# First attention batch: 512-query score tiles in single PSUM banks, remainders packed, row maxima over two banks

## The chip, the cores and the metric

One core of a Trainium2 chip runs the whole program. The metric is the device time of one execution in microseconds, the median over runs. The engines are named as the profile names them: PE (TensorE matmuls) with PEld (its weight loads), DVE (VectorE), ACT (ScalarE), POOL (GpSimd), SP (SyncE, which issues the DMAs). Each engine takes its instructions from one queue of its own, in order.

## What is computed

Thresholded attention over 4 batches, 8 heads, 576 positions and 64 dimensions, then two mixture-of-experts layers without routing, one after the other, over the 2304 positions.

```python
scores = scale * np.matmul(q, k.transpose(0, 1, 3, 2))
thresh = np.max(scores, axis=-1, keepdims=True) - tau
scores = np.where(scores >= thresh, scores, -1000000000.0)
scores = scores - np.max(scores, axis=-1, keepdims=True)
attn = np.exp(scores)
attn = attn / (np.sum(attn, axis=-1, keepdims=True) + 1e-09)
attn_out = np.matmul(attn, v)
...
h = x @ w_in                      # 512 -> 2048
g = P(h) / (Q(h) + 1e-06)         # cubic over quadratic in |h|
x = g @ w_out                     # 2048 -> 512
...
h = x @ w_in                      # second layer, 512 -> 2048
g = np.where(h >= 1, h, np.where(h <= -1, 0.0, (h + 1.0) ** 2 / 4.0))
out = g @ w_out
```

The weights arrive as 8-byte floats and have to be taken apart by integer instructions before they can be used.

## The kernel before

The program is a list of pieces of work, each with a priority (`at(when)`); a scheduler turns them into one fixed order for each engine. Three streams matter here.

**The first batch's attention** (`first_attention`, units at priorities -40 to -4). Heads are handled in four pairs. `prep_pair` loads and splits q and k of a pair into 16-bit halves and transposes them. `row_max` finds the largest score of each query: 128 queries by 512 keys per piece, two matmuls (L523, L524) into a PSUM bank and one DVE reduction (L527); then the rest pieces of 64 keys, then on nine columns the maximum is cut into three 16-bit pieces (`pcs`, L556), which PE transposes (L562) and ACT copies to `mrow` (L563). For pair 0 the pieces alternate between two PSUM tiles (tags `acc` and `s`); for the later pairs every piece uses the one bank `ph0`, and so do the three transposes. Then come nine score tiles per pair, keys on the partitions and all 576 queries along the row, as two halves of 288 in two banks (`transposed`): three matmuls per half (L579 to L581, the last of which subtracts the row maximum), an ACT instruction that marks what is under the threshold (L584, `low`), a matmul that subtracts the mark (L586), and the exponential (L587, `et`). Two score tiles exist (tags `s` and `acc`), each of two banks. The weighted sums of a tile (L596, two f32 matmuls, recorded as four) are issued one tile later, into the two banks `pv` and `ph1`; `take` copies them out in four or six ACT copies (L603, L604), and `divide` (L608 to L617) makes the result `xT` of the pair. The next pair's `row_max` is advanced beside the tiles, two units beside each of the first six tiles and one beside each of the others.

**The weights' conversion** (`convert`). 32 halves of weights, 16 for each layer, each 1 MB as read: a DMA into one of two `rw` buffers, three DVE instructions (L228 to L230), small matmuls for a bound (L253) with DVE and PE steps that make a scale (L254, L187, L188, L168 to L172), an ACT scaling and an ACT cast (L217, L208), four POOL subtractions (L212). The first layer's 16 halves have priorities -40 to -4, the second layer's 16 (`wh`) have -3 to 16.

**The layers** (`first_product`, `second_product`): 192 steps, 24 for each layer and batch, at priorities 0, 1, 2 and so on. One step is 24 matmuls (L846), some ten DVE and ACT instructions on 128 by 384 elements (`rational` L727 to L740 for the first layer, `quadratic` for the second), and three steps later 24 matmuls (L860). The first step needs `xT` of all four pairs. The attention of batches 1 to 3 (`attention`, scores L379 and L380, row instructions L425 and L387, sums L413) runs beside the steps, batch 1 from priority 16.5 on.

Eight PSUM banks exist: `aux`, `pv`, `ph0`, `ph1` (pool `ps_1`) and the two tiles of two banks `acc` and `s` (pool `ps_2`).

## Time and profile before

| what | us |
|---|---|
| runs: median (lowest to highest of 3) | 1267.02 (1266.43 to 1269.06) |
| the profiled execution's own time | 1266.28 |
| its span in the profile | 1264.5 |
| PE, PEld, DVE, ACT, POOL busy | 1096.8, 985.3, 1003.2, 824.5, 534.4 |
| last `xT` of the first batch written for step 0 (L617) | at 240.87 |

Times inside the program are counted from the start of the span. Busy time of an engine is what its instructions cover; the idle time of an engine that nobody waits for costs nothing, so each stage has to be read by itself. A granted clock of 1.00 is 2.4 GHz and one of 0.50 is 1.2 GHz; a mean between them is a mix of the two.

### The profile page before, as it was taken

The page shows a single profiled execution, that of the slowest core. Times are in us where ns is not written, and L with a number is a line of the kernel's source. Part 1 is how long each engine was busy: PE and PEld are TensorE (multiplying, and loading weights), DVE is VectorE, ACT ScalarE, POOL GpSimd, SP SyncE. Part 2 cuts the span into 40 slices and gives each one's busy share as a digit, 9 for nine tenths or more (in the row PEclk, how much of TensorE's full clock was granted, in tenths as well). Part 3 has the DMA queues.
Part 4 walks back from the last instruction along what each step waited for, and adds up shares of the span by engine and source line. Part 5 has one row for each costly group of instructions (what it writes and reads, how often), then busy time and mean ns, then how long its engine had stood idle before and what let it go on. Part 6 is the DMA issues. An engine that isn't in the chain of part 4 may idle for free.

```text
span 1264.5 us, 31682 instructions
## 1 busy us (share of the span) xinstructions
PE 1096.8 (87%) x12618; PEld 985.3 (78%) x12618; DVE 1003.2 (79%) x2371; ACT 824.5 (65%) x1473; POOL 534.4 (42%) x700
## 2 busy tenths in 40 slices
PE   2788778668788998999799999998889998999998
PEld 1454445567788887899688898997778998999997
DVE  7767977899997877789999766899997767897431
ACT  2476767668686677667676666777765766775332
POOL 3324546576553645421355454313454553222221
PEclk9797898779899999999999999999999999999999
DMA  7656657633427545933398548522784469006000
GB/s 206 221 171 213 231 193 248 239 114 98 117 73 234 114 98 100 241 124 84 73 225 193 94 91 205 178 53 58 214 185 76 102 148 243 14 2 237 32 14 26
DMA packets 220341, 176.40 MB, mean 139 GB/s; under 512 B 182048, under 2 KB 193312, under 8 KB 212000
## 3 DMA queue, kind: packets, MB, share of 16 engines
q1 hardware_dynamic: 220192, 174.36, 51.6%
q8 instruction: 99, 1.62, 0.5%
q14 instruction: 50, 0.41, 0.1%
HBM read 106.83 MB, written 21.50 MB: 101 GB/s over the span
## 4 chain that ended last, share of the span: by engine, by line
PE 37%; DVE 32%; DMA 11%; ACT 8%; issue 5%; POOL 5%; SPq 2%; DVEq 0%; ACTq 0%; POOLq 0%
PE ph L846 14%; PE acc L860 14%; DMA eT<-hl 6%; DVE e L387 3%; DVE sc L425 2%; PE pv L596 2%; DVE t L734 2%; DMA qkT<-qk 2%; PE pv L413 2%; DVE t L740 2%; DVE t L729 2%; DVE wt L229 2%; DMA rqk<-in_k_dram 2%; POOL hl L398 1%; DVE t L730 1%
## 5 line engine op out<-in xcount | busy, mean ns | idle before, releaser
L860 PE MATMUL acc<-gg,wc 128*128 128x192 f16 x4608 | 427.6, 247 | 16.7 <-DVE mye L188 8.4
L846 PEld LDWEIGHTS <-wc 128*128 128x128 f16 x4608 | 389.4, 99 | 30.0 <-DVE t L731 14.7
L860 PEld LDWEIGHTS <-wc 128*128 128x128 f16 x4608 | 383.7, 98 | 19.4 <-issue 17.8
L212 POOL TENSOR_TENSOR gg<-t,gg 128x384 f16<-128x384 f32 x192 | 187.6, 978 | 407.0 <-ACT gg L208 332.4
L846 PE MATMUL ph<-xT,wc 128*128 128x192 f16 x2304 | 220.1, 253 | 19.8 <-DVE t L731 15.3
L846 PE MATMUL ph<-yT,wc 128*128 128x192 f16 x2304 | 216.6, 246 | 2.3 <-DVE t L731 1.9
L398 POOL TENSOR_TENSOR hl<-e,hl 128x256 f16<-128x256 f32 x216 | 154.3, 735 | 0.0
L208 ACT CAST gg<-t 128x384 f16<-128x384 f32 x192 | 97.2, 508 | 83.9 <-DVE t L793 39.4
L387 DVE SCALAR_TENSOR_TENSOR e<-sc,nt,e 128x576 f32<-128x576 f32 x108 | 95.7, 886 | 33.0 <-ACT e L386 32.2
L792 DVE SCALAR_TENSOR_TENSOR t<-t,c 128x384 f32<-128x384 f32 x96 | 63.5, 662 | 72.6 <-ACT t L791 72.5
L386 ACT ACTIVATE e<-sc,nt,con 128x576 f32<-128x576 f32 x108 | 93.5, 866 | 7.2 <-POOL hl L398 0.2
L395 ACT CAST hl<-e 128x576 f16<-128x576 f32 x108 | 72.2, 669 | 35.6 <-DVE e L387 34.7
L727 ACT ACTIVATE t<-ph,sc 128x384 f32<-128x384 f32 x96 | 55.2, 575 | 60.8 <-PE ph L846 60.5
L791 ACT ACTIVATE t<-ph,c 128x384 f32<-128x384 f32 x96 | 64.0, 666 | 47.2 <-PE ph L846 46.7
L396 POOL TENSOR_TENSOR hl<-e,hl 128x64 f16<-128x64 f32 x108 | 40.0, 371 | 126.9 <-ACT hl L395 126.5
L413 PE MATMUL pv<-v,eT 128*128 128x65 f16 (+3 forms) x1680 | 70.7, 194 | 25.2 <-DMA eT<-hl 24.9
L425 DVE TENSOR_SCALAR_CACHE_REDUCE sc<-s 128x576 f32<-128x576 f32 x108 | 80.9, 749 | 13.3 <-PE s L380 12.8
L413 PEld LDWEIGHTS <-eT 128*128 128x128 f16 (+1 forms) x1680 | 62.9, 100 | 35.0 <-DMA eT<-hl 32.4
L732 ACT ACTIVATE t<-t,lc 128x384 f32<-128x384 f32 x96 | 67.9, 707 | 20.4 <-DVE t L729 19.8
L734 DVE SCALAR_TENSOR_TENSOR t<-t,ka,t 128x384 f32<-128x384 f32 x96 | 68.4, 713 | 13.9 <-ACT t L733 13.4
L212 POOL TENSOR_TENSOR wh<-wt,wh 128x256 f16<-128x256 f32 x64 | 60.6, 977 | 41.5 <-ACT wh L208 32.1
L212 POOL TENSOR_TENSOR wc<-wt,wc 128x256 f16<-128x256 f32 x64 | 55.4, 897 | 47.1 <-ACT wc L208 47.1
(233 smaller groups left out, 1901.5 us busy)
## 6 DMA issues: line engine op xcount, KB each, us to landing
wc<-scratch SPq DMA_DIRECT2D x56, 1024.0 KB, 5.9
rw<-in_moe_w_in_dram SPq DMA_DIRECT2D x16, 1024.0 KB, 5.9
rw<-in_moe_w_out_dram SPq DMA_DIRECT2D x16, 1024.0 KB, 5.6
scratch<-wc SPq DMA_DIRECT2D x8, 1024.0 KB, 5.8
scratch<-wh SPq DMA_DIRECT2D x16, 512.0 KB, 3.5
rqk<-in_q_dram SPq DMA_DIRECT2D x16, 256.0 KB, 3.0
rqk<-in_k_dram SPq DMA_DIRECT2D x16, 256.0 KB, 3.1
kT<-qkT SPq DMA_DIRECT2D x28, 144.0 KB, 2.4
```

What stands on the lines that cost most here:

```text
L208: A.copy(hi, src)
L212: G.tensor_tensor(lo[:, p], src[:, p], hi[:, p], op=ALU.subtract)
L386: A.activation(e, s, AF.Exp, bias=nb, scale=con[:, 0:1])
L387: V.scalar_tensor_tensor(e, s, th, e, op0=ALU.is_ge, op1=ALU.mult)
L395: A.copy(hi, e)
L398: G.tensor_tensor(lo_w[:, p], e[:, whole][:, p], hi[:, whole][:, p], op=ALU.subtract)
L413: T.matmul(pv[rows, 0:w], eT[:, c, cols], vv[:, h * NT + x if x < NT else H * NT + h, at : at + w], start=(n == 0), stop=(n == len(blocks) ...
L425: V.tensor_scalar(s, banks[:, 0:S], 1.0, -LARGEST, op0=ALU.mult, op1=ALU.max, accum_out=mx)
L732: A.activation(r, u, AF.Ln, bias=lc[:, 1:2], scale=lc[:, 0:1])
L734: V.scalar_tensor_tensor(s, s, ka[:, 0:1], r, op0=ALU.add, op1=ALU.mult)
L846: last = T.matmul(ph[:, f, :], w[:, wx, kt, f * P : (f + 1) * P], rhs, start=(n == 0), stop=(n == 3 * KT - 1))
L860: T.matmul(dst, w[:, wx, f, d * P : (d + 1) * P], gg[:, gx, f, :], start=(i == 0 and f == 0 and n == 0 and d % 2 == 0), stop=(i == NCH - 1 ...
```

## The change

Score tiles of the first batch now hold the first 512 queries in one bank. The last 64 queries of a head are computed for all its key tiles side by side in one bank, ahead of the nine main tiles (`_r` tiles: 320 columns for the first head, which carries the shared key tile, and 256 for the second). Their weighted sums go into the last 64 columns of that bank. The tags `s` and `acc` are taken once, as four banks: three rotate among the score tiles, the fourth serves `row_max`, which from pair 1 on alternates between it and `ph0`, the three transposes included. The weighted sums of the two heads go to `pv` and `ph1`, one bank each. A pair has ten program units in place of nine, so `N_FIRST` goes from 53 to 57.

```diff
         def bank(name):
-            if pr > 0:
-                return ps_1.tile([P, 512], F32, name=f"sm{pr}_{name}", tag="ph0")
             count[0] += 1
-            return ps_2.tile([P, 1024], F32, name=f"sm{pr}_{name}", tag="acc" if count[0] % 2 else "s")[:, 0:512]
+            if pr == 0:
+                return banks[count[0] % 4]
+            if count[0] % 2:
+                return banks[3]
+            return ps_1.tile([P, 512], F32, name=f"sm{pr}_{name}", tag="ph0")
...
-            pm = ps_1.tile([P, 512], F32, name=f"pmr{pr}_{c0}", tag="ph0")
+            pm = bank(f"m{c0}")
...
-    def transposed(pr, ab, t, data, n):
+    def transposed(name, parts, data, s):
...
+        w = sum(p[-1] for p in parts if p[1].start == 0)
+        for at, r, cols, c, of, n in parts:
+            dst, rhs = s[r, at : at + n], slice(of, of + n)
+            T.matmul(dst, kT[:, c, cols], q1[:, rhs], start=at == 0, stop=False, skip_group_check=True)
+            T.matmul(dst, kT2[:, c, cols], q1[:, rhs], start=False, stop=False, skip_group_check=True)
+            T.matmul(dst, less16[:, 0 : r.stop - r.start], mrow[:, rhs], start=False, stop=True, skip_group_check=True)
...
-        for z in range(2):
-            T.matmul(pv[z], w[r], e[r, z], start=first, stop=last)
+        T.matmul(pv, w[r], e[r], start=first, stop=last)
...
-        half = S // 2
-        for src, c0, c1, to in ((0, 0, ST, M), (0, ST, half, 0), (1, 0, half, half - ST)) if ab else ((0, 0, half, 0), (1, 0, half, half)):
-            c = slice(to, to + c1 - c0)
-            A.copy(d[h, c], pv[src][o, c0:c1])
-            A.copy(x[h, c], pv[src][h, c0:c1])
+        A.copy(d[h], pv[o])
+        A.copy(x[h], pv[h])
+
+    def rest(pr, e0, e1, pvs, vv, x, d):
+        for ab, dst in enumerate(pvs):
+            order = [NT, *range(NT)]
+            for n, t in enumerate(order):
+                e = e0 if ab == 0 or t == NT else e1
+                sums(dst, ab, pr, t, e[:, t * ST : (t + 1) * ST], vv, n == 0, n == NT)
+        for ab, pv in enumerate(pvs):
+            take(pv, ab, x[:, M:S], d[:, M:S])
...
+        two = [ps_2.tile([P, 1024], F32, name=f"front_{tag}", tag=tag) for tag in ("s", "acc")]
+        banks = [t[:, z * 512 : (z + 1) * 512] for t in two for z in range(2)]
...
+            for ab in range(2):
+                s = banks[n % 3]
+                pvs.append(s[:, M - ST : M])
+                n += 1
+                parts = sum((key_tile(ab, t, t * ST, 1) for t in range(NT + 1 - ab)), [])
+                es.append(transposed(f"{pr}_{ab}_r", parts, data, s))
+            held = [partial(rest, pr, *es, pvs, vv, x, d)]
+            next(rows, None)
+            yield
             for ab, t in [(0, t) for t in range(NT + 1)] + [(1, t) for t in range(NT)]:
-                e = transposed(pr, ab, t, data, n)
+                e = transposed(f"{pr}_{ab}_{t}", key_tile(ab, t, 0, 0), data, banks[n % 3])
...
-    N_FIRST = 17 + 9 * NP
+    N_FIRST = 17 + 10 * NP
```

What stands below are pieces of the fixed order of two engines. In the changed kernel the lines from 565 on are shifted: L565 is the `mrow` copy (was L563), L581 and L583 are `low` and `et` (were L584 and L587), L617 to L619 and L624 are `divide` (were L610 to L612 and L617).

ACT before, from the division of pair 0 (`rd_0`) to the first tile of pair 1 (`con_1` is a constant of pair 1; `wt` and `wc` are weights):

```order
L608 ACTIVATE rd_0_932<-d_0_594,least 128x576
L563 CAST mrow_262<-pmr_0_830 3x512
L217 ACTIVATE wt_3_0_722<-wt_3_0_722,pw_3_0_s 128x1024
L208 CAST wc_2_148<-wt_2_1_621 128x1024
L609 ACTIVATE rd_0_932<-rd_0_932 128x576
L217 ACTIVATE wt_3_1_879<-wt_3_1_879,pw_3_1_s 128x1024
L563 CAST mrow_262<-pmr_4_836 3x512
L208 CAST wc_3_149<-wt_3_0_722 128x1024
L208 CAST wc_3_149<-wt_3_1_879 128x1024
L563 CAST mrow_262<-pmr_8_842 3x128
L584 ACTIVATE low_0_0_954<-st_0_0_946,con_1_286 128x576
L584 ACTIVATE low_0_1_978<-st_0_1_970,con_1_286 128x576
```

ACT in the changed kernel, the same place, from the last `mrow` copy for pair 1 to the first tile of pair 1:

```order
L565 CAST mrow_262<-sm_m_793 3x128
L581 ACTIVATE low_1_1_842<-front_acc,con_0_175 128x512
L581 ACTIVATE low_1_2_852<-front_s,con_0_175 128x512
L208 CAST wc_2_148<-wt_2_1_659 128x1024
L217 ACTIVATE wt_3_0_798<-wt_3_0_798,pw_3_0_s 128x1024
L583 ACTIVATE et_1_1_841<-front_acc,con_0_175 128x512
L583 ACTIVATE et_1_2_851<-front_s,con_0_175 128x512
L217 ACTIVATE wt_3_1_859<-wt_3_1_859,pw_3_1_s 128x1024
L208 CAST wc_3_149<-wt_3_0_798 128x1024
L208 CAST wc_3_149<-wt_3_1_859 128x1024
L581 ACTIVATE low_1_3_893<-front_s,con_0_175 128x512
L581 ACTIVATE low_0_r<-front_acc,con_1_286 128x320
```

The `mrow` copies of pair 1 stood behind all of pair 0 and now stand ahead of its last three tiles; the first tile of pair 1 follows pair 0's last one directly, and the division of pair 0 comes behind it.

DVE before, the end of the first attention (`x_3` is pair 3's result; `wt_6_0` is a weight half of the second layer, the thirteenth of its sixteen) up to the first step's first instruction (L729):

```order
L188 TENSOR_REDUCE mw_5_0_3058<-pmmw_5_0_3059 128x1
L228 TENSOR_SCALAR wt_6_0_3304<-rw_6_0_3302 128x1024
L168 TENSOR_SCALAR f_w_137<-mw_5_0_3058 128x1
L617 SCALAR_TENSOR_TENSOR xT_0_258<-x_3_1612,v_s,xT_0_258 128x192
L229 SCALAR_TENSOR_TENSOR wt_6_0_3304<-rw_6_0_3302,wt_6_0_3304 128x1024
L617 SCALAR_TENSOR_TENSOR xT_1_259<-x_3_1612,v_s,xT_1_259 128x192
L171 TENSOR_SCALAR f_w_137<-f_w_137 128x1
L617 SCALAR_TENSOR_TENSOR xT_2_260<-x_3_1612,v_s,xT_2_260 128x192
L254 TENSOR_REDUCE mb_5_1_3145<-pg_5_1_3146 128x1
L230 SCALAR_TENSOR_TENSOR wt_6_0_3304<-rw_6_0_3302,wt_6_0_3304 128x1024
L172 RECIPROCAL pw_5_0_s<-f_w_137 128x1
L729 SCALAR_TENSOR_TENSOR t_0_0_0_1943<-t_0_0_0_1943,qc 128x384
```

DVE in the changed kernel, around the start of pair 3's division (`d_3`; `wt_7_1` is the last of all weight halves, `mv` belongs to the values of batch 1):

```order
L230 SCALAR_TENSOR_TENSOR wt_7_1_3570<-rw_7_1_3568,wt_7_1_3570 128x1024
L171 TENSOR_SCALAR f_w_137<-f_w_137 128x1
L300 TENSOR_REDUCE mv_3670<-rv_0_3671 128x1
L188 TENSOR_REDUCE mqke_0_3543<-pmmqke_0_3544 128x2
L617 SCALAR_TENSOR_TENSOR d_3_1544<-d_3_1544,rd_3_1786 128x576
L172 RECIPROCAL pw_7_0_s<-f_w_137 128x1
L259 TENSOR_REDUCE f_max_3448<-f_w_137 128x1
L159 TENSOR_SCALAR qk_0_f<-mqke_0_3543 128x2
L300 TENSOR_REDUCE mv_3670<-rv_1_3674 128x1
L254 TENSOR_REDUCE mb_7_1_3574<-pg_7_1_3575 128x1
L618 SCALAR_TENSOR_TENSOR d_3_1544<-d_3_1544,rd_3_1786 128x576
```

Before, the weight halves `6_0` (its last two instructions), `6_1`, `7_0` and `7_1` and the two L300 came behind the last `xT` of step 0; now all 32 halves and the L300 stand ahead of it.

## Rows read from the trace of the kernel before

**Rows 1.** Busy time by engine, granted clock and DMA around the first pair boundary.
```profile
92.00:105.00 13.00, 5.70 (x26) 2.53 (x23) 7.95 (x12) 12.60 (x20) 10.49 (x10) 0.59 0.66 194
```

**Rows 2.** The same view by stage: us, PE, PEld, DVE, ACT, POOL busy, PEclk, DMA, GB/s.
```profile
0.00:241.30 241.30, 164.42 (x986) 103.86 (x987) 185.50 (x404) 148.46 (x232) 110.54 (x133) 0.86 0.66 215
241.30:330.70 89.40, 63.95 (x622) 59.74 (x622) 86.33 (x174) 66.12 (x113) 52.97 (x56) 0.83 0.44 135
330.70:378.10 47.40, 42.65 (x532) 41.47 (x530) 45.76 (x104) 36.95 (x71) 26.30 (x27) 1.00 0.22 67
378.10:447.20 69.10, 62.27 (x812) 57.08 (x810) 54.13 (x145) 41.77 (x79) 32.05 (x48) 1.00 0.65 164
```

**Rows 3.** DVE's waits from 50 to 241.3: for whom, us in total, times, longest.
```profile
DVE wt L228 <- POOL wc L212: 7.7, 7, 2.5
DVE mw L188 <- PE pmmw L187: 6.2, 6, 2.3
DVE mx L527 <- PE sm L524: 5.6, 4, 3.4
...
DVE mb L254 <- PE pg L253: 3.9, 4, 1.5
...
DVE d L610 <- ACT rd L609: 3.5, 1, 3.5
DVE mx L527 <- PE sm_t L524: 3.0, 2, 2.5
DVE mx L527 <- PE sm_rt L524: 1.6, 2, 1.2
```

**Rows 4.** DVE by line, 50 to 241.3: count, busy us, mean ns of one, idle before.
```profile
L230 DVE SCALAR_TENSOR_TENSOR wt<-rw,wt 128x1024 int32<-128x1024 int32 x24 | 34.4, 1434 | 0.2
L229 DVE SCALAR_TENSOR_TENSOR wt<-rw,wt 128x1024 int32<-128x1024 int32 x25 | 32.8, 1310 | 0.2
L228 DVE TENSOR_SCALAR wt<-rw 128x1024 int32<-128x1024 int32 x25 | 19.1, 762 | 17.0 <-POOL wc L212 7.7 <-POOL wh L212 4.8 <-DMA rw<-in_moe_w_out_dram 3.6
L188 DVE TENSOR_REDUCE mw<-pmmw 128x1 f32<-128x128 f32 x23 | 6.5, 284 | 6.2 <-PE pmmw L187 6.2
...
L168 DVE TENSOR_SCALAR f_w<-mw 128x1 int32<-128x1 int32 x23 | 3.4, 149 | 0.4
```

**Rows 5.** DVE by line, 241.3 to 378.1, the same columns.
```profile
L300 DVE TENSOR_REDUCE mv<-rv 128x1 f32<-128x2048 f32 x2 | 4.5, 2272 | 0.0
...
L387 DVE SCALAR_TENSOR_TENSOR e<-sc,nt,e 128x576 f32<-128x576 f32 x4 | 3.2, 803 | 0.0
L425 DVE TENSOR_SCALAR_CACHE_REDUCE sc<-s 128x576 f32<-128x576 f32 x4 | 3.0, 745 | 0.0
...
L300 DVE TENSOR_REDUCE mv<-rv 128x1 f32<-128x512 f32 x2 | 1.3, 668 | 0.0
```

**Rows 6.** PE by line, 378.1 to 447.2 (attention of batch 1).
```profile
L413 PE MATMUL pv<-v,eT 128*128 128x65 f16 (+3 forms) x168 | 7.6, 194 | 5.1 <-DMA eT<-hl 5.1
L379 PE MATMUL s<-qkT 128*128 128x512 f16 (+3 forms) x26 | 6.9, 287 | 1.5 <-DVE sc L425 1.5
L380 PE MATMUL s<-kT,qkT 128*128 128x512 f16 (+3 forms) x26 | 5.3, 286 | 0.0
```

**Rows 7.** Timeline of DVE and ACT: start, us, instruction, idle before.
```profile
53.19 1.35 ACT L584 ACTIVATE low<-st,con 128x576 bf16<-128x576 f32 x2
...
197.22 1.37 ACT L584 ACTIVATE low<-st,con 128x576 bf16<-128x576 f32 x2
...
230.80 0.78 ACT L608 ACTIVATE rd<-d,least 128x576 f32<-128x576 f32 x1
...
240.87 0.41 DVE L617 SCALAR_TENSOR_TENSOR xT<-x,v_s,xT 128x192 f16<-128x192 f32 x1
```

**Rows 8.** ACT by line, 25 to 245: the two instructions of a score tile.
```profile
L584 ACT ACTIVATE low<-st,con 128x576 bf16<-128x576 f32 x36 | 25.7, 734 | 21.2 <-PE st L581 21.1
L587 ACT ACTIVATE et<-st,con 128x576 f32<-128x576 f32 x36 | 25.4, 738 | 9.3 <-PE st L586 9.3
```

More of the change, by code (lines that the diff above doesn't have):

```diff
@@ L507, in first_v, with row_max @@
         return vv
-    def row_max(pr, qT, kT, kT2, mrow):
+    def row_max(pr, qT, kT, kT2, mrow, banks):
         k1 = kT.rearrange("p c s -> p (c s)")
@@ L564, in row_max @@
         yield
-    def transposed(pr, ab, t, data, n):
+    def transposed(name, parts, data, s):
         con, qT, kT, kT2, mrow = data
-        name = f"{pr}_{ab}_{t}"
-        s = ps_2.tile([P, 1024], F32, name="st" + name, tag="acc" if n % 2 else "s")
-        s = s.rearrange("p (z n) -> p z n", z=2)[:, :, 0 : S // 2]
         q1 = qT.rearrange("p c s -> p (c s)")
-        tiles = [(ab, slice(0, P), slice(0, P), ab * (NT + 1) + t)]
-        if t == NT:
-            tiles = [(i, slice(i * ST, (i + 1) * ST), slice(i * ST, (i + 1) * ST), NT) for i in range(2)]
-        for i, r, cols, c in tiles:
-            for z in range(2):
-                dst, of = s[r, z], slice(i * S + z * S // 2, i * S + (z + 1) * S // 2)
-                T.matmul(dst, kT[:, c, cols], q1[:, of], start=True, stop=False)
-                T.matmul(dst, kT2[:, c, cols], q1[:, of], start=False, stop=False)
-                T.matmul(dst, less16[:, 0 : r.stop - r.start], mrow[:, of], start=False, stop=True)
-        e = mp.tile([P, 2 * W], F32, name="et" + name, tag="tp", bufs=N_TEMP)[:, 0:S].rearrange("p (z n) -> p z n", z=2)
-        low = mp.tile([P, 2, S // 2], BF16, name="low" + name, tag="poly", bufs=N_POLY)
@@ L584, in transposed @@
+        e = mp.tile([P, 2 * W], F32, name="et" + name, tag="tp", bufs=N_TEMP)[:, 0:w]
+        low = mp.tile([P, 2 * W], BF16, name="low" + name, tag="poly", bufs=N_POLY)[:, 0:w]
         A.activation(low, s, AF.Relu, bias=con[:, 3:4], scale=-STEEP)
-        for z in range(2):
-            T.matmul(s[:, z], minus, low[:, z], start=False, stop=True, skip_group_check=True)
+        T.matmul(s, minus, low, start=False, stop=True, skip_group_check=True)
         A.activation(e, s, AF.Exp, scale=con[:, 0:1])
@@ L588, in transposed, with key_tile @@
         return e
+    def key_tile(ab, t, at, part):
+        n, of = (M, (0, S + ST)) if part == 0 else (ST, (M, S))
+        if t < NT:
+            return [(at, slice(0, P), slice(0, P), ab * (NT + 1) + t, of[ab], n)]
+        return [(at, slice(i * ST, (i + 1) * ST), slice(i * ST, (i + 1) * ST), NT, of[i], n) for i in range(2)]
     def sums(pv, ab, pr, t, e, vv, first, last):
@@ L633, in first_attention @@
         yield
-        for _ in row_max(0, *pairs[0][1:], mrows[0]):
+        two = [ps_2.tile([P, 1024], F32, name=f"front_{tag}", tag=tag) for tag in ("s", "acc")]
+        banks = [t[:, z * 512 : (z + 1) * 512] for t in two for z in range(2)]
+        for _ in row_max(0, *pairs[0][1:], mrows[0], banks):
             yield
@@ L641, in first_attention @@
             data = *pairs[pr], mrows[pr % 2]
-            rows = row_max(pr + 1, *pairs[pr + 1][1:], mrows[(pr + 1) % 2]) if pr + 1 < NP else iter(())
+            rows = row_max(pr + 1, *pairs[pr + 1][1:], mrows[(pr + 1) % 2], banks) if pr + 1 < NP else iter(())
             x = ap.tile([P, S], F32, name=f"x0_{pr}", tag="e", bufs=N_SC)
             d = ap.tile([P, S], F32, name=f"d0_{pr}", tag="sc", bufs=N_SC)
-            held = []
+            es, pvs = [], []
+            for ab in range(2):
[7 more added lines that the diff above has]
+            yield
             for ab, t in [(0, t) for t in range(NT + 1)] + [(1, t) for t in range(NT)]:
-                e = transposed(pr, ab, t, data, n)
+                e = transposed(f"{pr}_{ab}_{t}", key_tile(ab, t, 0, 0), data, banks[n % 3])
+                n += 1
                 for f in held:
@@ L650, in first_attention @@
                 if t == 0:
-                    pv = [ps_1.tile([P, 512], F32, name=f"pv{z}_{pr}_{ab}", tag=tag)[:, 0 : S // 2]
-                          for z, tag in enumerate(("pv", "ph1"))]
+                    pv = ps_1.tile([P, 512], F32, name=f"pv{pr}_{ab}", tag="ph1" if ab else "pv")
                     held = [partial(sums, pv, 1, pr, NT, tail, vv, True, False)] if ab else []
@@ L655, in first_attention @@
                 elif t == NT or (ab and t == NT - 1):
-                    held = [partial(sums, pv, ab, pr, t, e, vv, False, True), partial(take, pv, ab, x, d)]
+                    held = [partial(sums, pv, ab, pr, t, e, vv, False, True), partial(take, pv, ab, x[:, 0:M], d[:, 0:M])]
                     tail = e
@@ L659, in first_attention @@
                     held = [partial(sums, pv, ab, pr, t, e, vv, False, False)]
-                for _ in range(2 if n % 9 < 6 else 1):
+                for _ in range(2 if 5 * ab + t < 6 else 1):
                     next(rows, None)
-                n += 1
                 yield
```

2 lines of the change are left out of this document (1 added, 1 removed).

## The prediction

> **What bounds the kernel now.** The change touches only the first batch's attention, so I read the stages first [rows 2]. Up to 241.3 us no engine is full: DVE is the busiest with 185.5, PE has 164.4, ACT 148.5. From there to 330.7, the first fourteen layer steps, DVE is busy for 86.3 of 89.4, and to 378.1, where step 24 begins, for 45.8 of 47.4. From 378.1 to 447.2 it is PE, 62.3 of 69.1 at full clock (2.4 GHz), while DVE has 54.1. So the time is made by three things in a row: how early the first batch's `xT` is done (240.87 [rows 7]), then DVE's work, then PE's work. In the first stage I then asked what DVE waits for [rows 3]. From 50 us on (up to there both orders of DVE are alike, row for row) the rows shown come to 31.5 us. The reader should see three kinds: row maxima that wait for their scores (5.6, 3.0 and 1.6, together 10.2), the division that waits for ACT (3.5), and the rest in the weights' conversion (POOL 7.7 and more, PE round trips 6.2 and 3.9). The change can take away the first two; the conversion stays as it is.
>
> **The change part by part, the cheap parts.** Score matmuls, weighted sums and marks cover the same columns in fewer, longer instructions, but for the packed remainders. Those have 30 score matmuls of 64 columns per pair. PE idles 241.3 - 164.4 = 77 us in this stage, so I cost this at nothing; if that cover were gone, the 120 small matmuls at the 0.19 us of a recorded small matmul [rows 6] would be 23 us at most. ACT gets four more tile instructions per pair (two of 320 and two of 256 columns), and its other eighteen shrink from 576 to 512. One of 576 takes 0.73 us [rows 8], so the sixteen added ones cost between nothing and 16 x 0.73 = 12 us; fewer `take` copies give some of it back. ACT idles 93 us in the stage [rows 2], so this too is nothing on the path.
>
> **The order.** What moves is larger than what is added. Row maxima through two banks let the next pair's maximum finish early: ACT's copies of `mrow` for pair 1 now stand ahead of pair 0's last three tiles, where they stood behind pair 0. At that boundary PE was busy for 5.7 of 13 us and its granted clock was 0.59 [rows 1]; that hole should close. But the scheduler has also put more conversion in front: DVE gets its first `xT` of pair 3 for step 0 after all 32 weight halves, where before four halves came later. I count DVE's rows between row 97 of its order and that `xT`. Added are four L230 (1.434), four L229 (1.310) and three L228 (0.762), five pairs of L254 and L188 (0.284 each; I take the two as equal), fifteen scale steps of 0.149 [rows 4], two L300 (2.272 and 0.668) [rows 5], and some ten tiny ones at 0.15: 5.7 + 5.2 + 2.3 + 2.8 + 2.2 + 2.9 + 1.5 = 22.6 us. All of it lies in DVE's queue ahead of the end of the first attention, and DVE is the fullest engine, so it counts in full.
>
> Against it stands the idle time that is recovered, D. Bounds: nothing, if DVE merely waits at its next row; or the 13.7 of row maxima and division together with the 10.1 of PE round trips, 24 in all. Below nothing too: the four extra halves bring their own waits, and new ones may appear. I take 10, three quarters of the 13.7, because the waits removed are those of one bank used in turn, and pair 0's maxima already alternate. So step 0 starts at 240.9 + 22.6 - 10 = 253.5, about 13 us **later** than now.
>
> The 24 steps of the first layer then lose those 22.6 us of DVE work. They gain five rows of batch 1's attention, which now precede step 24: 5 x (0.803 + 0.745) [rows 5] and small instructions, 10 us by my count. 137.2 us (240.9 to 378.1) become 137.2 - 22.6 + 10 = 124.6, and step 24 begins at 378.1, as now. But PE has by then done 24 score matmuls and 68 sums of batch 1 which it did later, in the stage that it bounds: 24 x 12.2/52 + 68 x 7.6/168 = 8.7 us [rows 6], of which I count PE's busy share there, 0.9: 7.8 us. From step 36 on both orders are alike. The sum is D - 22.6 + 22.6 - 10 + 7.8 = D - 2.2, a **gain of 7.8 us** with D = 10. Of the profiled execution's 1266.3 that leaves 1258.5. The runs' median is 0.7 above that execution, which is less than the runs' own spread.
>
> A conversion's price itself moves with its neighbours. L230 and L229 average 1.434 and 1.310 in this stage although they do the same amount of work on the same shapes [rows 4]. The Trainium skill says that GpSimd shares its SBUF interfaces with VectorE and contends with DVE instructions in a two-port mode or with two SBUF inputs (GPSIMD Engine Reference, section 8, Key points). By that rule the packed conversions would be dearer ahead of step 0 and the steps behind them cheaper, and the sum would stay where it is.
>
> **Rivals.**
> - *The idle time only changes its place.* DVE's order is fixed; a reduction that no longer waits leads at once to a conversion row that waits for POOL or PE [rows 3]. For: such waits are more than half of the 31.5 us. Against: the boundary hole, where ACT and PE are held up too. D is then near 2 and the time 1266. Chance 0.20.
> - *The attention ends late: slower.* After pair 3's `mrow` the new ACT order has four tiles of pair 2 and eleven of pair 3 to go, where nine were. Those nine took from 197.2 to 230.8 [rows 7], 3.7 us each; 13 full and two small ones at that pace are 52 us, and with `mrow` at 197 and 10 us of division the start is at 259 at the latest. But over the whole stage the 36 tiles went at 4.9 us (from 53.2 to 230.8 [rows 7]); at that pace it is 69 us, the start is at 276, D is -12 and the sum +14.6: 1281. It decides from a start of step 0 at 264 on. For: DVE's extra rows lie among these tiles, and every engine waits on another in a fixed order. Against: tiles have three banks to rotate in instead of two. Chance 0.17.
> - *The clock falls more often.* The granted clock is 0.86 over the stage [rows 2] and 0.59 where PE has holes [rows 1]. If many short waits at bank changes held it at 0.59, PE's 164 us would be 164 x 0.86/0.59 = 240 of the 254, the 10 would not be recovered and the PE round trips of 10.1 would grow by half: D = -5 and the sum +7, and with new waits for PE up to +14; I take 1277. Chance 0.08. The Trainium skill describes such a thing: a kernel with 512-column matmuls that cycles through PSUM banks in each iteration leaves PE short idle moments between groups, and its clock swings between the two levels (TensorE: Matmul & The Clock Gate, "A second HAM failure mode: psum-queue depth-cycling"). That speaks against this change, which rotates through three banks; whether this trace agrees cannot be read before, since its tiles alternate as well.
> - *More is recovered.* With the boundary holes closed, the clock stays at 2.4 GHz there and the PE round trips shrink too: D near 20, 1248.5. Chance 0.12.
> - That the change doesn't do what it says can be left out: the orders show the banks and the moved rows.
>
> **How the numbers follow.** The forecast case has the remaining 0.43. About 2.5 us (0.2%) is what a measurement of this kernel can tell from no change. Faster by more than that: the forecast and the case of more recovered, 0.55. Within: 0.20. Slower: 0.17 + 0.08 = 0.25. The forecast's own range, D from 5 to 16, is 1252 to 1264. The range for 8 in 10 reaches to D = 24 at one end (1244.5, say 1245) and to most of the slower cases at the other (1279).
>
> **What would show it.** In the changed kernel: DVE's waits for the scores of row maxima down from 10.2 to a few us and the division's 3.5 gone; the hole around 92 to 105 filled, its clock above 0.59; step 0's `xT` between 247 and 262, later than 240.9, with no weight conversion behind it; 24 steps in some 125 us; step 24 near 378; and from step 36 on a lead of about 8 us that stays to the end. It is wrong if step 0 starts after 264, or if it starts no later than now, or if DVE is not full in the 24 steps, so that the work moved ahead was not on the path there.

## The result and the profile after

| | before | after |
|---|---|---|
| median of the runs, us | 1266.72 (1260.64 to 1269.06, 4 runs) | 1281.88 (1279.46 to 1284.24, 4 runs) |
| ratio to before, 95% interval | | 1.0137 [1.0107, 1.0167] |
| profiled execution, own time / span, us | 1266.28 / 1264.5 | 1280.81 / 1279.0 |

The changed kernel is slower by 1.4%. The forecast was 1258.5 with a range up to 1279, so the time lies outside of it; it is within 1 us of the rival in which the attention ends late (1281).

First the stages, in the view of [rows 1, 2]. The first line is the old hole at the first pair boundary, the next end at the first layer step, at step 14, at step 24 and at step 36 of the changed kernel (us, then PE, PEld, DVE, ACT and POOL busy, granted clock, DMA share, GB/s):

```profile
92.00:105.00 13.00, 8.23 (x65) 3.85 (x64) 12.07 (x19) 9.24 (x15) 6.76 (x9) 1.00 0.79 282
0.00:269.30 269.30, 177.57 (x1008) 96.65 (x1009) 203.27 (x451) 161.04 (x252) 126.30 (x153) 0.87 0.66 217
269.30:348.20 78.90, 62.50 (x671) 56.94 (x670) 78.39 (x168) 63.32 (x118) 43.09 (x50) 0.90 0.36 91
348.20:394.20 46.00, 43.36 (x530) 41.99 (x528) 42.10 (x95) 36.80 (x72) 28.00 (x28) 1.00 0.22 63
394.20:457.90 63.70, 58.40 (x732) 55.09 (x730) 44.51 (x117) 33.31 (x64) 23.98 (x33) 0.97 0.59 154
```

The hole is filled, as forecast: DVE 12.07 of 13 us where it had 7.95, PE at 2.4 GHz where the mean granted clock was 0.59 [rows 1]. Yet the first stage is 28 us longer [rows 2] and the next three are 17.3 us shorter in all (78.9, 46.0 and 63.7 for 89.4, 47.4 and 69.1). Steps are counted from 0. Step 0's first matmuls run early, with the first pairs' `xT`, so the start of the steps is read from step 1: by the first matmul of each, step 1 starts at 269.8 (241.9 before), step 24 at 394.2 (378.1), step 36 at 457.9 (447.2).

DVE's waits up to there, in the view of [rows 3] (who waits for whom, us in total, times, longest):

```profile
DVE mw L188 <- PE pmmw L187: 10.6, 9, 3.1
DVE mx L529 <- PE sm L526: 8.3, 4, 4.5
DVE wt L228 <- POOL wh L212: 7.8, 7, 2.0
DVE mb L254 <- PE pg L253: 5.0, 6, 2.8
DVE wt L228 <- POOL wc L212: 4.0, 6, 1.1
DVE wt L228 <- DMA rqk<-in_k_dram: 3.9, 1, 3.9
...
DVE mx L529 <- PE front_acc L526: 3.8, 3, 2.0
...
DVE mv L300 <- DMA rv<-in_v_dram: 2.5, 1, 2.5
```

The wait of the division is gone, but the row maxima (mx) wait 8.3 + 3.8 us where they waited 10.2, and the conversions' PE round trips (mw, mb) 15.6 where they waited 10.1. Two waits for loads are new, 3.9 (k) and 2.5 (batch 1's V). Outside these waits DVE did 167.9 us of work from 50 us to step 1, before 149.8: 18.1 us more (counted as 22.6), with 51.9 us of idle time where there were 42.1.

The chain of tiles shows where the start went. From ACT's timeline (start, us, instruction): the last row of pair 3's `mrow`, the first tile behind it, the stretch around pair 3's packed tiles, the last tile and the division.

```profile
179.38 0.25 ACT L565 CAST mrow<-sm_m 3x128 f16<-3x128 f32 x1
181.96 0.69 ACT L581 ACTIVATE low<-front_acc,con 128x512 bf16<-128x512 f32 x1 [0.72 <-PE front_acc L577]
...
207.33 0.68 ACT L583 ACTIVATE et<-front_acc,con 128x512 f32<-128x512 f32 x1
217.49 0.69 ACT L581 ACTIVATE low<-front_s,con 128x512 bf16<-128x512 f32 x1 [4.01 <-PE front_s L577]
...
250.03 0.67 ACT L581 ACTIVATE low<-front_s,con 128x512 bf16<-128x512 f32 x1
251.53 0.69 ACT L583 ACTIVATE et<-front_s,con 128x512 f32<-128x512 f32 x1
257.37 0.77 ACT L615 ACTIVATE rd<-d,least 128x576 f32<-128x576 f32 x1
```

`mrow` is done 17.6 us earlier than before (179.6 against 197.2 [rows 7]), as the order promised. But the 15 tiles behind it take from 179.6 to 257.4: 77.7 us, 5.2 each. The longest gap without a tile's instruction on ACT runs from 208.0 to 217.5. PE's timeline says what it did there:

```profile
207.49 5.09 PE L597 MATMUL front_s<-et_r,v 64*128 64x64 f32 x20 [1.06 <-ACT et_r L583]
212.37 2.02 PE L597 MATMUL pv<-et,v 128*128 128x512 f32 x2
214.19 0.63 PE L575 MATMUL front_acc<-qT,kT 128*128 128x512 f16 x1
```

The pair's ten small weighted sums, 20 passes of float32 (two are recorded for each matmul), come in one block of 5 us, and the next score tile stands behind it in PE's queue. By form (count, busy us, mean ns), all of the first attention's sums, first in the changed kernel:

```profile
L597 PE MATMUL pv<-et,v 128*128 128x512 f32 x64 | 39.2, 697 | 3.5 <-ACT et L583 3.5
L597 PE MATMUL front_s<-et_r,v 128*128 128x64 f32 x48 | 10.9, 403 | 0.0
L597 PE MATMUL pv<-et,v 64*128 64x512 f32 x16 | 5.6, 641 | 0.0
L597 PE MATMUL front_s<-et_r,v 64*128 64x64 f32 x12 | 3.5, 386 | 2.0 <-ACT et_r L583 1.4 <-ACT et L583 0.6
L597 PE MATMUL front_acc<-et_r,v 128*128 128x64 f32 x16 | 2.2, 281 | 0.0
L597 PE MATMUL front_acc<-et_r,v 64*128 64x64 f32 x4 | 0.9, 296 | 0.1
```

and in the kernel before:

```profile
L596 PE MATMUL pv<-et,v 128*128 128x288 f32 x128 | 42.6, 454 | 1.4 <-ACT et L587 1.4
L596 PE MATMUL pv<-et,v 64*128 64x288 f32 x32 | 10.9, 442 | 0.1
```

The sums cost 62.3 us of PE where they cost 53.5, for the same columns and the same number of passes: 160 before, and 80 wide and 80 small ones after. The mean lengths are no price of a pass, because the records overlap and mix two clocks. PE's loads show the clock (same columns):

```profile
L597 PEld LDWEIGHTS pv<-et,v 128*128 128x128 f32 x64 | 12.0, 214 | 10.2 <-ACT et L583 6.6 <-issue 1.8
L597 PEld LDWEIGHTS front_s<-et_r,v 128*128 128x128 f32 x48 | 9.9, 304 | 0.7
L597 PEld LDWEIGHTS front_acc<-et_r,v 128*128 128x128 f32 x16 | 1.9, 191 | 0.1
```

The last two lines are the same load for the same small sums, 304 ns and 191. What differs is when they ran. By block of small sums (us, PE and PEld busy in them, granted clock, DMA share, GB/s; pair 0, pair 2 in two halves, pair 3):

```profile
59.23:64.20 4.97, 4.94 (x20) 4.40 (x20) 0.52 1.00 370
153.70:155.20 1.50, 1.49 (x11) 1.42 (x12) 1.00 0.08 10
156.65:158.20 1.55, 1.47 (x10) 1.26 (x10) 1.00 1.04 407
207.45:212.60 5.15, 5.11 (x21) 4.76 (x22) 0.50 0.61 216
```

Ten passes take 1.5 us at 2.4 GHz, and twenty take 4.9 to 5.1 at 1.2 GHz. Ahead of the last block PE was busy for 1.0 of 4.6 us (202.8 to 207.4), with the clock already at 0.50. Sorted by the granted clock, PE is busy for 0.311 us a pass over 288 columns at full clock (146 passes), 0.496 over 512 (69) and 0.147 over 64 (30), and for 0.251 over 64 at half clock (46). From these an estimate at full clock throughout is 49.8 us for the sums before and 51.4 after: of the 8.8 us the split itself is worth under 2, and the rest is the lower clock, which 50 of the 80 small passes met in whole or in part (and 11 of the 80 wide ones; before, 14 of 160).

A small pass is dear for its width all the same. At full clock one follows the next after 112 ns, where 64 of the 288 columns of a pass that takes 242 ns would be 54. The likely reason is the weights, which each pass loads anew: the loads follow each other after 108 to 112 ns too. No run tests it. The Trainium skill says that a load's time goes by the stationary operand's columns; by its formula an estimate for 128 columns is 107 ns (TensorE: Matmul & The Clock Gate, LDWEIGHTS). The trace agrees in the pace at full clock, not in the recorded length of one load, 183 to 192 ns there, since the records overlap; at half clock the pace is 213 ns.

### The profile page after: what moved, and what is told of

Same layout as the page of the kernel before. It is cut to its first block, busy times and chain, and to the rows that moved or that the text cites. A ratio compares the mean times of both kernels' runs of the same rounds, so it can differ in the third digit from the quotient of the medians.

```text
span 1279.0 us, 31657 instructions
## 1 busy us (share of the span) xinstructions
PE 1106.8 (87%) x12590; PEld 974.1 (76%) x12590; DVE 1002.3 (78%) x2371; ACT 824.4 (64%) x1481; POOL 534.8 (42%) x700
## 4 chain that ended last, share of the span: by engine, by line
PE 34%; DVE 29%; DMA 13%; ACT 7%; POOL 7%; issue 7%; SPq 2%; DVEq 0%; ACTq 0%; POOLq 0%
PE acc L877 14%; PE ph L863 13%; DMA eT<-hl 7%; DVE e L387 3%; DVE sc L425 2%; POOL hl L398 2%; DVE t L746 2%; DVE t L751 2%; DMA qkT<-qk 2%; PE pv L413 2%; POOL wc L212 2%; DVE t L757 2%; DVE t L747 1%; DVE t L748 1%; POOL wh L212 1%
## 5 line engine op out<-in xcount | busy, mean ns | idle before, releaser
L863 PEld LDWEIGHTS <-wc 128*128 128x128 f16 x4608 | 388.8, 99 | 27.9 <-DVE t L748 12.0
L863 PE MATMUL ph<-xT,wc 128*128 128x192 f16 x2304 | 218.1, 251 | 15.2 <-DVE t L748 12.7
L413 PE MATMUL pv<-v,eT 128*128 128x65 f16 (+3 forms) x1680 | 71.5, 195 | 24.8 <-DMA eT<-hl 24.6
L751 DVE SCALAR_TENSOR_TENSOR t<-t,ka,t 128x384 f32<-128x384 f32 x96 | 68.1, 710 | 12.9 <-ACT t L750 12.3
L379 PE MATMUL s<-qkT 128*128 128x512 f16 (+1 forms) x240 | 64.2, 292 | 15.3 <-DVE sc L425 15.2
L212 POOL TENSOR_TENSOR wh<-wt,wh 128x256 f16<-128x256 f32 x64 | 57.8, 933 | 44.2 <-ACT wh L208 38.2
```

What stands on the lines that cost most here:

```text
L212: G.tensor_tensor(lo[:, p], src[:, p], hi[:, p], op=ALU.subtract)
L413: T.matmul(pv[rows, 0:w], eT[:, c, cols], vv[:, h * NT + x if x < NT else H * NT + h, at : at + w], start=(n == 0), stop=(n == len(blocks) ...
L751: V.scalar_tensor_tensor(s, s, ka[:, 0:1], r, op0=ALU.add, op1=ALU.mult)
L863: last = T.matmul(ph[:, f, :], w[:, wx, kt, f * P : (f + 1) * P], rhs, start=(n == 0), stop=(n == 3 * KT - 1))
```

## The experiments

Theory A: the packed tiles (A1: their own round trip, A2: their small sums) lengthen the chain of tiles. Theory B: the order that the scheduler made of the change, with more of DVE's rows ahead of step 0, costs time by itself. Against both: the row maxima in two banks.

Ratios are to the kernel before, with 95% intervals. The columns of times and the columns on PE come from one profiled execution each; PE's run from 50 us to the first matmul of step 36, and idle is that length less PE's busy time, so with like busy times it says no more than when step 36 begins. "Ahead" counts the conversions of weight halves in front of the last `xT` on DVE.

| kernel | ahead | step 1 at | step 36 at | PE busy | PE idle | ratio |
|---|---|---|---|---|---|---|
| before | 28 | 241.9 | 447.2 | 312.4 | 84.8 | |
| **after** | 32 | 269.8 | 457.9 | 323.5 | 84.4 | 1.0137 [1.0107, 1.0167] |
| after_norest | 29 | 243.5 | 443.8 | 309.9 | 83.9 | 0.9959 [0.9928, 0.9991] |
| after_nosums | 29 | 240.1 | 439.1 | 309.8 | 79.3 | 0.9946 [0.9921, 0.9972] |
| nosums_hold4 | 28 | 246.4 | 443.7 | 309.1 | 84.6 | 0.9980 [0.9958, 1.0003] |
| after_hold4 | 28 | 245.0 | 442.9 | 321.0 | 71.9 | 1.0039 [1.0008, 1.0069] |
| after_ph0 | 30 | 246.1 | 444.9 | 323.2 | 71.7 | 1.0053 [1.0023, 1.0083] |
| ph0_hold4 | 28 | 245.5 | 448.9 | 320.7 | 78.2 | 1.0070 [1.0044, 1.0096] |
| after_holdL300 | 31 | 260.1 | 451.6 | 328.8 | 72.8 | 1.0048 [1.0031, 1.0065] |
| after_holdV | 32 | 267.7 | 455.4 | 324.3 | 81.1 | 1.0138 [1.0116, 1.0161] |
| after_hold1 | 31 | 271.4 | 458.5 | 327.2 | 81.3 | 1.0147 [1.0125, 1.0168] |
| after_hold2 | 30 | 264.1 | 458.4 | 325.8 | 82.6 | 1.0154 [1.0111, 1.0197] |
| after_hold8 | 24 | 245.9 | 457.6 | 327.6 | 80.0 | 1.0159 [1.0132, 1.0187] |
| before_all32 | 32 | 262.8 | 457.2 | 317.0 | 90.2 | 1.0090 [1.0062, 1.0118] |
| before_hold8 | 24 | 230.4 | 451.7 | 312.7 | 89.0 | 1.0068 [1.0044, 1.0091] |
| spread2_hold4 | 28 | 266.7 | 465.0 | 322.9 | 92.1 | 1.0205 [1.0175, 1.0235] |
| conv2_hold4 | 28 | 289.4 | 485.4 | 339.7 | 95.7 | 1.0368 [1.0327, 1.0409] |

**The packed tiles left out, or their sums alone.**

```
-            held = [partial(rest, pr, *es, pvs, vv, x, d)]
+            held = []
+            G.memset(x[:, M:S], 1.0)
+            G.memset(d[:, M:S], 1.0)
```

This is after_nosums; after_norest drops the loop that fills `es` as well.

> The changed kernel without the tiles of the 64 last queries: the eight packed score tiles, their 40 weighted sums and their 16 copies are left out, and these queries' part of x and d is filled with 1.0, so the output differs. Theory A (each tile of the first attention costs a round trip of some 4.8 us whatever its width, and the change has 44 tiles where there were 36): the first layer step, at 269.8 us in the changed kernel and 241.9 before, starts at 232 to 240, and the time falls below that of the kernel before, to 1255 to 1262. Theory B (the rest tiles are cheap; the late start comes from the order, four conversions and two V loads ahead of step 0): the start falls only by what the order gives back, to 250 to 260, and the time stays at 1272 or more.

> The changed kernel with the eight packed score tiles kept, but without their weighted sums (40 matmuls of 64 columns) and the 16 copies behind them; x and d of these queries are filled with 1.0, so the output differs. Theory A in its plain form (the cost is the tile's own round trip: scores, cut, marks, exponential): little changes, the start stays at 260 or later and the time at 1274 or more. Theory A2 (the cost is the chain of small float32 sums and the copies that ACT waits for, 5 to 9 us per pair): the start falls to 240 to 250 and the time to 1258 to 1268. Theory B (the order): as for the kernel without rest tiles, 250 to 260 and 1272 or more.

Medians 1258.50 and 1258.42, both faster than the kernel before and both 1.8% to 1.9% faster than the changed kernel. The two medians are alike, which speaks for the sums and copies (A2) against the packed tiles' own round trips (A1). But the order had changed as well: without the sums the scheduler puts 29 conversions ahead and no V load, so this pair does not separate A2 from B.

**The order put back.** DVE's part of the last four halves, and of batch 1's attention, is queued behind the last `xT`:

```
-                with at(t - 3):
+                with at(t - 3), tc.issue_after(done[0]) if 2 * u[1] + u[2] >= 12 else nullcontext():
                     stage_half(1, u[1], u[2], False)
...
-                with at(t - 1.5):
+                with at(t - 1.5), tc.issue_after(done[0]):
                     next(atts[u[1]])
```

> The changed kernel with the order put back at its end: DVE's subtractions of the last four halves of the second layer, and those of batch 1's attention, are queued behind the last xT of the first attention, so 28 conversions stand ahead of step 0 as in the kernel before. Theory A (the tiles): the start moves forward by about the 22.6 us of work taken away, to 245 to 252, the 24 steps take that work back, and the time stays within 4 us of the changed kernel, 1278 to 1285. Theory B (the order, with the waits that each conversion brings): the start falls to 242 or earlier and the time to 1266 to 1270.

Median 1269.36: the order carries 1% of the 1.4%, by theory B's number. The start of the steps, 245.0, is by theory A's. Stage by stage (same columns as above):

```profile
50.00:245.00 195.00, 150.87 (x864) 80.51 (x863) 144.04 (x312) 135.15 (x216) 95.02 (x108) 0.87 0.66 227
245.00:376.30 131.30, 109.02 (x1161) 103.18 (x1160) 121.32 (x255) 99.52 (x177) 71.55 (x70) 0.90 0.33 95
376.30:442.90 66.60, 61.10 (x815) 56.33 (x812) 58.75 (x164) 41.65 (x82) 35.63 (x52) 1.00 0.80 179
```

The steps up to 24 take 131.3 us where the changed kernel needs 124.4, those to 36 take 66.6 for 63.7. So of the 24.8 us that the start gains, 9.8 are given back. The rows behind step 24 ran where DVE has room (58.75 of 66.6 us, against 44.51 of 63.7 in the changed kernel).

With the sums left out as well, at the same 28 conversions:

> As the earlier kernel without the small weighted sums (left out with their copies, these queries' x and d filled with 1.0), but with the order held at 28 conversions, so that beside the changed kernel with four held (1269.4 us) only the sums and copies differ. If the sums are dear by themselves: 1255 to 1262, start of the steps at 232 to 240. If the 11 us between the kernel without sums and the one with four held came from their orders (29 conversions against 28): 1265 to 1271.

Median 1259.72, ratio 0.9980 against 1.0039: by the medians the sums and copies cost 0.6%, some 7 us, at a like order. The two intervals, [0.9958, 1.0003] and [1.0008, 1.0069], only just part. The profiled executions do not show it: step 36 begins at 443.7 without the sums and at 442.9 with them, and the executions took 1267.06 us (the slowest of its ten) and 1266.26. PE is busy for 11.9 us less without the sums, and idle for 12.7 us more. The kernel before does these sums too, inside its 288-column passes, so 7 us would be the price of the work and not of the split.

What the change costs against the kernel before, at the same number of conversions, is after_hold4's 1.0039, 0.1% to 0.7%. Up to step 36 that kernel is not late but 4.3 us early (442.9 against 447.2): PE is busy for 8.6 us more and idle for 12.9 us less. The lead is lost in steps 96 to 104 (last section).

**The order alone, in the kernel before.** Pair 3's division is queued behind the last conversion:

```
-            divide(pr, x, d)
+            if pr == NP - 1:
+                for n in range(2 * NCH):
+                    with at(WEIGHTS[0] + n * (WEIGHTS[1] - WEIGHTS[0]) / (2 * NCH) - 3):
+                        stage_half(1, n // 2, n % 2, False)
+            with tc.issue_after(lastconv[0]) if pr == NP - 1 else nullcontext():
+                divide(pr, x, d)
...
-    spread(*WEIGHTS, [("w", i, x) for i in range(NCH) for x in range(2)])
```

> The kernel before, its tiles unchanged, with one edit: the division of pair 3 is queued on DVE behind the second layer's last conversion, so that all 32 conversions stand ahead of step 0 as in the changed kernel (28 before); the two V loads' maxima stay behind. If the order alone costs the 12 us that putting it back in the changed kernel gave: the start of the first layer step moves from 242 to 255 to 265 and the time rises by 7 to 13 us (ratio 1.006 to 1.010). If the order costs only together with the rest tiles that lie among the conversions: the steps give the work back and the time stays within 4 us of before.

Median 1273.62, +0.9%: this order costs without any packed tile. Other than expected, the first two V maxima stand ahead as well (at 256.44 and 259.56, the last `xT` at 262.41), as in the changed kernel. Step 1 moves by 20.9 us, step 36 by 10.0; in the changed kernel it was 27.9 and 10.7.

**Is it the number of conversions?** Eight halves held instead of four (the index 12 in the diff becomes 8), in both kernels:

> The kernel before with eight of the second layer's halves queued behind the last xT: 24 conversions ahead of step 0 where there were 28. If each conversion ahead of step 0 costs time at the end (3 us each by the changed kernel's 12 us for four of them and two loads): the start falls to 225 to 232 and the time by 6 to 12 us (ratio 0.990 to 0.995). If DVE, full in the first fourteen steps, takes as long for them there: the time stays within 4 us of before; slower by 3 or more if the second layer then waits for its weights at step 24.

> The changed kernel with eight of the second layer's halves queued behind the last xT: 24 conversions ahead of step 0 where there were 32 (28 with four held, 1269.4 us). If each costs at the end: start at 228 to 235 and a time of 1256 to 1263. If the steps take them back in full: 1266 to 1273, as with four held.

No: 1271.48 and 1283.81, slower than with 28. In the kernel before, step 1 moved 11.5 us forward to 230.4, and the steps gave back more than that. In the changed kernel it did not move (245.9 with 24, 245.0 with 28): there the tiles, not DVE, set the end of the attention, and DVE waits once for 29.1 us for the division's `rd`.

**Which row?** Four variants of the diff of after_hold4. after_holdL300 has its second edit alone. after_hold1 and after_hold2 have the first alone, with the index 15 and 14. after_holdV moves the two V maxima and nothing else:

```
-            V.tensor_reduce(mx[:, g : g + 1], raw.rearrange("p t d -> p (t d)"), axis=AX.X, op=ALU.max,
+            with tc.issue_after(done[0]) if b == 1 else nullcontext():
+                V.tensor_reduce(mx[:, g : g + 1], raw.rearrange("p t d -> p (t d)"), axis=AX.X, op=ALU.max,
```

> The changed kernel with nothing held but the V loads' maxima of batch 1 and the rows behind them (two of 2.27 and 0.67 us, which stood ahead of step 0); 31 conversions stay in front. If the conversions carry the cost of the order: 1276 to 1283. If the V loads do (they wait for a transfer of 3.9 us besides): 1268 to 1274.

> The changed kernel with one thing moved: the two maxima of batch 1's V load, which stand ahead of and inside pair 3's division, are queued behind the last xT; all 32 conversions and batch 1's q and k rows stay where they are. If the wait for the V load (2.48 us) and the maximum of 2.29 us, in front of a division whose operand was there, carry the cost: the start falls from 269.8 to 262 to 265 and the time to 1271 to 1276. If the small q and k rows and the 32nd conversion between the division's rows carry it: 1278 to 1283.

> The changed kernel with the second layer's last half alone queued behind the last xT: 31 conversions ahead, batch 1's q and k rows and the first V maximum still among the rows of pair 3's division. If the 32nd conversion carries the cost: 1268 to 1274, as with batch 1's rows held (1270.1). If batch 1's rows do: 1278 to 1284.

> The changed kernel with the second layer's last two halves queued behind the last xT: 30 conversions ahead, and batch 1's rows fall behind step 0 with them. By both theories 1266 to 1273, as with 31 and batch 1's rows held (1270.1) and with 28 (1269.4); a time between 1274 and 1280 would say that the cost grows with each conversion ahead, and that 1270 at 31 was chance.

1270.13, 1282.12, 1281.44 and 1283.71. The first said that the conversions are neutral and that batch 1's rows cost 12 us. The second shows that the suspect in front of the division is not it. In DVE's timeline of the changed kernel (start, us, instruction, idle before) it sat idle for a transfer, though `rd` had been there since 258.9:

```profile
261.20 2.29 DVE L300 TENSOR_REDUCE mv<-rv 128x1 f32<-128x2048 f32 x1 [2.48 <-DMA rv<-in_v_dram]
263.40 0.41 DVE L188 TENSOR_REDUCE mqke<-pmmqke 128x2 f32<-128x256 f32 x1
263.73 0.75 DVE L617 SCALAR_TENSOR_TENSOR d<-d,rd 128x576 f32<-128x576 f32 x1
```

and with the V maxima moved the division did start 3.3 us earlier, in the same view:

```profile
259.99 0.42 DVE L188 TENSOR_REDUCE mqke<-pmmqke 128x2 f32<-128x256 f32 x1
260.47 0.76 DVE L620 SCALAR_TENSOR_TENSOR d<-d,rd 128x576 f32<-128x576 f32 x1
```

Yet the time stayed at 1282: this wait looked like a large part of the delay, and taking it away was worth nothing that can be measured. The last two runs refute the first reading as well. Holding two halves also puts batch 1's q and k rows and the V maxima behind step 0, and brings nothing. So none of the rows tried carries it alone, and the cost is not monotone in what is held. What goes with the time, among kernels with the same work, is PE's idle time up to step 36: 72 to 73 us in the three kernels of the change at 1.004 to 1.005, 78 at 1.007, and 80 to 84 in the five at 1.014 to 1.016; in the kernel before 84.8, and 89 and 90 where it became slower. That is the cost itself as PE meets it, and no cause. Which waits make those 10 us in one order and not in the next stays open.

**Two banks for the row maxima.** They go back to one:

```
-            if count[0] % 2:
-                return banks[3]
             return ps_1.tile([P, 512], F32, name=f"sm{pr}_{name}", tag="ph0")
```

> The changed kernel with the row maxima of pairs 1 to 3 in one bank, as before: the part of the change on the row maxima undone, the tiles as changed. If the two banks recover idle time of the attention (the forecast's 10 us of row-max waits): start later than 269.8 by 5 to 12 us less what the order moves, and the time 1285 to 1292. If the row maxima are not on the chain that ends last (theories A and B): the time stays within 4 us of the changed kernel, 1278 to 1286.

> Row maxima of pairs 1 to 3 in one bank, tiles as changed, and the order held at 28 conversions, so that it stands beside the changed kernel with four held (1269.4 us) and differs by the two banks alone. If the two banks recover the row-max waits (the forecast's 10 us, or a part): 1274 to 1280. If the maxima are not on the chain that ends last: 1266 to 1273.

With one bank the kernel is not slower but faster, 1271.22. The scheduler then leaves 30 conversions and no V load ahead, but that alone is not the reason: after_hold2 has two banks and also 30 conversions and no V load ahead, and stands at 1.0154. At 28 conversions in both, one bank stands at 1.0070 and two at 1.0039, with intervals that overlap: two banks are worth between nothing and some 4 us, not 10. The scores' waits are alike: 12.6 us with one bank (10.0, 2.1 and 0.5), 9.6 with two (7.5 and 2.1).

**Attempts at a faster version.** The small sums spread, each behind the wide sum of its key tile, with an accumulator in `ph0` and two banks for the tiles:

```
+    def few(rp, ab, pr, t, er, vv, last):
...
+        T.matmul(rp[:, ab * ST : (ab + 1) * ST], w.rearrange("p x d -> p (x d)")[r], e[r],
+                 start=ab == 0 and t == 0, stop=last, skip_group_check=True)
...
-                e = transposed(f"{pr}_{ab}_{t}", key_tile(ab, t, 0, 0), data, banks[n % 3])
+                e = transposed(f"{pr}_{ab}_{t}", key_tile(ab, t, 0, 0), data, banks[n % 2])
```

> The changed kernel with four halves held, and the small weighted sums no longer in one block at a pair's start: each stands behind the wide sum of the same key tile, in a bank of its own (ph0), and their copies at the heads' ends; tiles then rotate in two banks, row maxima in the two others. If the block and ACT's wait for it cost the time: start at 235 to 241 and 1258 to 1264, faster than the kernel before. If the 80 recorded passes of some 0.4 us cost wherever they stand, or two banks are too few: 1267 to 1275.

1290.86: a miss. DVE waits for the division's `rd` once for 22.1 us, with all 28 conversions done. Since the third bank went at the same time, whether the spread sums or the two banks did it is not separated. Then, with the row maxima back in one bank and four halves held, the bank that this leaves free as a second one for the first layer's conversions:

```
+    def spot(m, i, x, name):
+        if m == 1 and 2 * i + x >= 0:
+            return None
+        return ps_1.tile([P, 512], F32, name="pm" + name, tag="ph0")
...
-        s = root("pw" + name, f_w[m][x][:, i : i + 1], everywhere("mw" + name, bound, 1), 2.0**64, even=m == 1 and x == 1)
+        s = root("pw" + name, f_w[m][x][:, i : i + 1], everywhere("mw" + name, bound, 1, place=spot(m, i, x, name)), 2.0**64, even=m == 1 and x == 1)
```

> The changed kernel with four halves held and row maxima of pairs 1 to 3 in one bank (ratio 1.007 in the run of that kernel), and now the transposed maxima of the first layer's 16 conversions written to the bank that this leaves free, ph0, where all conversions used one bank for their Gram sums and their maxima. If the conversions' turn in one bank paces the tiles, since each tile's relu stands on ACT behind a conversion's scaling: the start falls from 245.5 to 230 to 240 and the time to 1256 to 1264, faster than the kernel before. If the pace comes from elsewhere (the conversions' own round trips over DVE, PE, ACT and POOL): 1268 to 1276.

1309.78: a worse miss, since a second bank for the conversions did not quicken the tiles among them. But it measures the tiles alone. DVE is through with its conversions early and waits for the last tiles of the attention; from 262 to 282 us nothing but tiles runs (us, then PE, PEld, DVE, ACT, POOL):

```profile
262.00:282.00 20.00, 14.54 (x46) 4.94 (x46) 0.00 (x0) 11.27 (x18) 0.00 (x0) 1.00 0.00 0
```

and ACT's timeline has the first and the last row of the eight wide tiles in it:

```profile
261.77 0.69 ACT L584 ACTIVATE low<-front_s,con 128x512 bf16<-128x512 f32 x1 [3.91 <-PE front_s L580]
...
280.88 0.69 ACT L586 ACTIVATE et<-front_s,con 128x512 f32<-128x512 f32 x1 [0.47 <-PE front_s L585]
```

Eight tiles in 19.8 us are 2.5 us each. after_hold8 agrees: its last eight, behind its 24 conversions, take from 218.3 to 238.0, 19.7 us. Among conversions the 15 tiles of the changed kernel take 5.2 (above), and those of the kernel before took 4.9 over the first stage. So a tile alone takes about half of the time. Not all of the difference need be the conversions': in these stretches there are also no row maxima and no small sums, and the clock is 1.00 in them, where it was 0.87 over the changed kernel's first stage. In the orders a tile's relu stands on ACT behind a conversion's scaling, which waits for DVE, which waits for PE; that this is how the two hold each other up is not shown.

No version tried beats the kernel before and computes everything; the two that are faster leave the small sums out.

## Why the prediction failed

- **Holes and row maxima.** Right about the order (`mrow` 17.6 us earlier) and the boundary (DVE 12.07 of 13 us). Wrong in what it is worth: the row maxima still wait 12.1 us, and at 28 conversions they wait 9.6 us with two banks and 12.6 with one. Only the division's 3.5 us went.
- **D, the recovered idle time.** This step failed most. It was put at +10 (bounds 0 to 24, "below nothing too"); DVE's idle time ahead of step 1 grew from 42.1 to 51.9, D = -9.8. The growth is in the conversions' PE round trips (5.5 us more), the two new waits for loads (6.4) and the row maxima (1.9), against the division's 3.5 that went. The 22.6 us of added DVE work were 18.1. Step 1 was forecast 12.6 us later and came 27.9 later: 15.3 us. The forecast took the order as neutral (22.6 us ahead, 22.6 us saved behind) but for D. The runs give it a price: the same 32 conversions ahead cost the kernel before 0.9%, and with four held behind step 0 the changed kernel's 1.4% falls to 0.4%. Which wait of that order carries it, and why holding one, two or eight brings nothing, stays open.
- **Small sums "at nothing".** The text priced the packed score matmuls and let the sums pass as covering the same columns in fewer instructions; they are 160 passes before and after. Both were to lie in PE's 77 us of idle time. The sums cost 8.8 us more of PE's time, most of it by the lower clock. Whether idle time covers added work depended on the order: in the changed kernel PE is busy for 11.1 us more up to step 36 and its idle time is what it was (84.4 for 84.8), but at 28 conversions it is busy for 8.6 us more and idle for 12.9 us less. So the cover was there, and failed only together with the order.
- **The 24 steps.** Right: 124.4 us for 124.6 (0.8 short of the forecast gain, counted from step 1), with DVE busy for 120.0 of it and nine of batch 1's rows where there were four.
- **Steps 24 to 36.** Right in kind: 63.7 for 69.1, a gain of 5.4 where 7.8 was put, 2.4 short.
- **The lead stays to the end.** Wrong by 3.8: it is lost between steps 96 and 104 (last section). Together 15.3 + 0.8 + 2.4 + 3.8 = 22.3, which is the forecast's gain of 7.8 and the loss of 14.5 between the two profiled executions.
- **The rivals.** The late attention had the trigger (a start after 264), the trailing tiles (15) and their pace (4.9; measured 5.2) right. It got 1281 by D = -12, so its size is partly chance: D was -9.8, and the rest came from terms that it did not have. It also put pair 3's `mrow` at 197 and the tiles at 69 us, where 179.6 and 77.7 were measured. It took the tile pace as given; some other orders of the same tiles give 1269 to 1272.
- **The clock.** Its mean did not fall: 0.87 over the stage, 0.86 before. The slow stretches lie elsewhere, on the small sums above all, where the text had put nothing. The cycling rule of the Trainium skill that the rival named (TensorE: Matmul & The Clock Gate, "A second HAM failure mode: psum-queue depth-cycling") has no support in this mean.

## What to carry to other kernels

Before a mean length is taken as a price, see at which clock its instructions ran and whether they overlap: here the same small sums took PE 0.147 us a pass at full clock and 0.251 at half, and most of what looked like the price of splitting a tile was the clock. Idle time of an engine may cover added work in one order and not in another: with 28 conversions ahead PE took the added sums out of its idle time, with 32 it did not. Where a scheduler makes the order, test a change with the order held as well as free: here the same tiles gave 1.004 to 1.016 by what stood ahead of step 0, and one run of one order would have named the wrong row.

## What the runs showed that was not expected

Steps 96 to 104 take 42.9 to 44.5 us in all 13 kernels with packed score tiles and 38.9 to 39.4 in the four without, far from the code that differs. In the changed kernel PE's waits there have one long wait for a transposing transfer, where it was 1.0 us before:

```profile
PE pv L413 <- DMA eT<-hl: 4.1, 1, 4.1
```

One of these transfers took 9.0 us from issue to landing, before at most 6.3. SyncE's order is the same there. In after_hold4 these steps take 44.1 us, 5.0 more than in the kernel before, which is all of its lead of 4.3 us at step 36 and more; so this loss weighs as much as all that the tiles cost at a like order. Why the tiles of the first attention have a part in it was not tried and stays open.

Fewer conversions ahead of step 0 are not better, nor are more: in the kernel before 24 cost 0.7% and 32 cost 0.9% against the scheduler's 28.
